# Attention and mixture of experts on one core: the second half of k is prepared one tile later, and the mask product reads PSUM

## The chip, the cores and the metric

The kernel runs on one core of a Trainium2 chip. The metric is the device time of one execution in microseconds (us).

The engines are named as the profile names them. PE is TensorE, DVE is VectorE, ACT is ScalarE, POOL is GpSimd, and SP is the engine whose queue issues most of the DMAs.

## The reference

Four batches, eight heads, 768 positions and 64 numbers a head go through local attention, and the result through a mixture of four experts.

```python
scores = scale * np.matmul(q, k.transpose(0, 1, 3, 2))          # q, k, v: (4, 8, 768, 64)
keep = is_global | is_local                                     # 8 first positions, or 96 behind
scores = np.where(keep, scores + bias, -1000000000.0)
a = softmax(scores)
x = (a @ v) as (4 * 768, 512)
p = domain_probs / (domain_probs.sum(-1, keepdims=True) + 1e-09)
for e in range(4):
    h = np.maximum(x @ w1[e], 0.0)                              # 512 -> 1024
    out += p[:, e:e + 1] * (h @ w2[e])                          # 1024 -> 512
```

## The kernel before

**The stages.** The attention of batch 0 runs first. Then the experts of batches 0 and 1 run (`first` and `second`), and beside them the attention of batches 1, 3 and 2 (`attention_chain`), whose instructions are put between those of the experts. From about 705 us on only the experts of batches 2 and 3 are left (`late_batch`).

**The unit of attention.** `attention_chain` goes through 12 pairs of heads, four for each of its three batches. A pair has six tiles of 128 queries. The chain is a generator that yields after each step, and a line near the end of the kernel (`count, span = ...`) paces it: the steps are spread evenly over the steps of the experts. A step is a call of `flow`, which is a pipeline four tiles deep. A tile enters with its scores (`scores`, four products into a tile of `ps`); one step later comes its softmax up to the exponential, and two steps later its normalisation to `pn` (both in `softmax`); three steps later it is turned (`turn_folded`: two or three transposes of `pn` into a PSUM tile `pt`, which are then copied to `pT` in SBUF). Once the sixth tile of a pair has been turned, the next step multiplies all six `pT` with v and vg (`weigh`, twice: 10 products into one `pt` tile for tiles 0 to 2, and 12 into another for tiles 3 to 5, each copied out by ACT as `x` or `piece`). There are 22 such products a pair, each half as wide as the array; they are counted here as 44, as the trace counts them.

**Other uses of `pt`.** q and k of a pair come in halves of three tiles. `prepare_q` and `prepare_k` transpose a half into a `pt` tile (three transposes), ACT copies it out and DVE takes what is left of it. The half of k with tiles 3 to 5 is needed from the scores of tile 3 on. All of this shares two PSUM buffers: `pt` has `bufs=2`, and the results of `weigh` lie in the same pool.

**The order.** While the attention chain runs, the framework's scheduler may reorder the instructions of each engine (`Ordered.on = False`); it works from its own costs. On the chip each engine then takes its own instructions strictly in that order, and a semaphore wait holds all that stands behind it.

**The experts.** `first` makes seven products (`pm<-xT,w1s`, `pm<-xB,w1s`, six matmuls of 384 columns each) for a unit of hidden features, and `second` six (`pm<-w2s,h`, six matmuls of 512 columns each). DVE adds them up, ACT makes the ReLU (`h`). The weights of a unit come by DMA (`raw`), and ACT and POOL split them into high and low parts (`w1s`, `w2s`); for batch 0 POOL also makes sums of them.

Of the kernel before, what the change touches and what calls it, by code (L numbers as in the profile page):

```python
# [14 lines left out]
ALU = mybir.AluOpType  # L15
# [3 lines left out]
P = 128  # L19
# [3 lines left out]
NPREV = 96  # L23
# [163 lines left out]
def attn_moe_kernel(ctx: ExitStack, tc, q, k, v, n_global, n_local, domain_probs, w1, w2, out):  # L187
# [4 lines left out]
    NQT = S // P  # L192
    NPAIR = H // 2
# [16 lines left out]
    ve, ac, po, sy, te = (Ordered(tc, e) for e in (nc.vector, nc.scalar, nc.gpsimd, nc.sync, nc.tensor))  # L210
# [11 lines left out]
    LATE = 2  # L222
# [9 lines left out]
    newer = fast.tile([P, P + NGLOB], BF16, name="newer")  # L232
# [177 lines left out]
    def scores(A, t, got):  # L410

        both = A.ps.tile([P, 2, 2 * P], F32, name="ps")
        c0 = (NQT - 1 - t) * PL - (0 if t else NPREV)
        for j in range(2):
            win = got["k"][:, j].rearrange("p t c -> p (t c)")[:, c0 : c0 + 2 * P]
            for part in range(2):
                te.matmul(
                    both[:, j],
                    got[("q", t // TPH)][:, j, part, t % TPH * P : (t % TPH + 1) * P],
                    win,  # L420
                    start=(part == 0),
                    stop=(part == 1),
                )
        return both
# [93 lines left out]
    def turn_folded(A, tile_):  # L518

        t, pn = tile_["t"], tile_["pn"]  # L520
        pt = A.pt.tile([P, 4, P], F32, name="pt")
        pT = tile_["pT"] = A.pT.tile([P, 2, 2, P], F32, name="pT")
        for place, at in enumerate((0, PL + NGLOB, P)[: 3 if t else 2]):
            te.transpose(pt[:, place, :], pn[:, at : at + P], ident)
        if t:
            for j in range(2):
                ac.copy(pT[NPREV:, 0, j], pt[j * NGLOB : (j + 1) * NGLOB, 2])
        ac.copy(pT[:, 1], pt[:, :2])
        if t:
            ve.scalar_tensor_tensor(  # L530
                pT[:NPREV, 0], newer[:NPREV, None, :P].to_broadcast([NPREV, 2, P]), 1.0, pT[:NPREV, 1],
                op0=ALU.subtract, op1=ALU.mult,
            )

    def weigh(A, three, x, b):

        px = A.px.tile([P, 512], F32, name=A.pxname)
        for i, tile_ in enumerate(three):
            t, pr, pT = tile_["t"], tile_["pr"], tile_["pT"]
            vt, vg = tile_["v"]["v"], tile_["v"]["vg"]  # L540
            parts = (1,) if t == 0 else (0, 1) if A.early else (1, 0)
            for w in parts:
                for j in range(2):
                    vv = vt[:, j, t] if w == 1 else vg[:, j, t - 1]
                    te.matmul(
                        px[j * D : (j + 1) * D, i * P : (i + 1) * P],
                        vv,
                        pT[:, w, j, :],
                        start=(w == parts[0]),
                        stop=(w == parts[-1]),  # L550
                    )
        cols = slice((t - TPH + 1) * P, (t + 1) * P)
        if x is not None:
            ac.copy(x[:, pr, cols], px[:, :HALF])
        else:
            piece = A.st.tile([P, HALF], F32, name="piece")
            ac.copy(piece, px[:, :HALF])
            ac.dma_start(xd[b][:, pr, cols], piece)
# [84 lines left out]
    def attention_chain(bs, A):  # L643

        tiles, turned = [None] * 4, []
        order = [(b, pr) for b in bs for pr in PAIRS]
        nats, gots = [{} for _ in order], [{} for _ in order]

        def flow(new=None):

            one, two, three, four = tiles
            if new:
                new["both"] = scores(A, new["t"], gots[new["m"]])
                new["ps"] = [new["both"][:, j] for j in range(2)]
            if four:
                turned.append(four)
            if len(turned) == NQT:
                b = order[four["m"]][0]
                for half in (turned[:TPH], turned[TPH:]):
                    weigh(A, half, xs[b], b)  # L660
                turned.clear()
            if three:
                turn_folded(A, three)
            softmax(A, one, two)
            tiles[:] = [new, one, two, three]

        def fetch_heads(m, names):

            if m < len(order):
                for n in names:  # L670
                    nats[m][n] = next(load(A, {"q": q, "k": k, "v": v}[n], *order[m], n))

        fetch_heads(0, "qkv")
        yield
        prepare_q(A, nats[0]["q"], 0, gots[0])
        flow()
        yield
        spread_q(0, gots[0])
        for m, (b, pr) in enumerate(order):
            if pr == PAIRS[0]:  # L680
                xs[b] = None if b == B - 1 else xp.tile([P, NPAIR, S], F32, name="x")
                if b == B - 1:
                    xd[b] = dp.tile([P, NPAIR, S], F32, name="x_last")
            nat, got = nats[m], gots[m]
            for part, hf in ((prepare_k, 0), (prepare_q, 1)):
                part(A, nat[part.__name__[-1]], hf, got)
                flow()
                yield
            for t in range(NQT):
                if t == 1:  # L690
                    prepare_k(A, nat["k"], 1, got)
                if t == 4 and m + 1 < len(order):
                    prepare_q(A, nats[m + 1]["q"], 0, gots[m + 1])
                if t in (1, 2, 4):
                    flow()
                    if t == 2 and m:
                        fetch_heads(m, "v")
                    yield
                flow({"t": t, "pr": pr, "m": m, "v": nat})
                if t == 0:  # L700
                    spread_q(1, got)
                elif t == 1:
                    fetch_heads(m + 1, "q")
                elif t == 3:
                    fetch_heads(m + 1, "k")
                elif t == 4:
                    if m + 1 < len(order):
                        spread_q(0, gots[m + 1])
                    nat["vg"] = differences(A, nat["v"])
                yield  # L710
        while any(tiles):
            flow()
            yield
# [201 lines left out]
    per = E * NPR  # L915
# [524 lines left out]

    SUMUNITS = tuple(per + i for i in (0, 1, 3, 4, 5, 7, 8, 9, 11, 12, 13))
    todo_t = [units[i][1:] for i in range(per)]
    count, span = 3 * NPAIR * (5 + NQT) + 6, (LATE * 13 * per - 12) * 0.97
    emitted = done = paced = 0
    Ordered.on = True
    for _ in first_sums(1):
        work_chores()
    chores.append(first_splits())
    att = attention_chain((1, 3, 2), A)
    begin = 30  # L1450
    for b in range(LATE):
# [89 lines left out]
```

## Time and profile before

| | |
|---|---|
| median of 3 runs | 1172.14 us (1171.06 to 1173.47) |
| the profiled execution | 1172.39 us, its span 1170.6 us |
| PE busy | 1141.7 us, 98% of the span |
| DVE, ACT, POOL busy | 887.0, 635.9, 628.8 us |
| granted PE clock over the span | 0.997 |

The span runs from the first to the last instruction that the profile shows; 1.8 us of the profiled execution lie around it. The ends of PE's matmuls are modelled, so a busy PE may still be waiting; the starts of the matmuls are what is read below.

### The profile page before, as it was taken

The numbers are of one execution on the slowest core, as the hardware profiler recorded it, in microseconds if no ns is written. First come the engines' busy times: TensorE is split into PE (matmuls) and PEld (weight loads), VectorE is DVE, ScalarE is ACT, GpSimd is POOL, SyncE is SP. The second block draws the span as 40 slices with busy tenths as digits, with TensorE's granted clock in tenths as the row PEclk, the third lists the DMA queues.
The fourth block names the chain that finished last, engine by engine and source line by source line (L and its number), as shares of the span: only waits on it lengthen the run. The fifth ranks groups of instructions, "written<-read, shape, count | busy, mean of one in ns | idle before, by whom it ended". The sixth has DMA issues, their size and how long they took to land.

```text
span 1170.6 us, 21402 instructions
## 1 busy us (share of the span) xinstructions
PE 1141.7 (98%) x7414; PEld 1054.6 (90%) x7414; DVE 887.0 (76%) x2065; ACT 635.9 (54%) x1801; POOL 628.8 (54%) x609
## 2 busy tenths in 40 slices
PE   7899899999999999999999999999999999999997
PEld 5679788988888989888888989999999999999997
DVE  7977678777868877887787677777777777777776
ACT  6844777777753656666575324444444544444443
POOL 5676555645543224313222337777877855555554
PEclk9999999999999999999999999999999999999999
DMA  9558868678786898968857668888888687776763
GB/s 185 147 156 284 289 194 309 235 228 237 249 280 227 271 257 278 278 220 257 260 187 238 224 217 311 306 302 304 294 295 293 236 297 244 249 251 243 248 229 132
DMA packets 180978, 290.80 MB, mean 248 GB/s; under 512 B 86784, under 2 KB 137472, under 8 KB 168576
## 3 DMA queue, kind: packets, MB, share of 16 engines
q1 hardware_dynamic: 172992, 273.63, 70.3%
q10 hardware_dynamic: 7872, 15.74, 4.5%
q8 instruction: 61, 1.00, 0.4%
q14 instruction: 53, 0.43, 0.1%
HBM read 207.93 MB, written 70.78 MB: 238 GB/s over the span
## 4 chain that ended last, share of the span: by engine, by line
PE 80%; DVE 7%; ACT 6%; POOL 3%; issue 2%; DMA 2%; ACTq 0%; SPq 0%; DVEq 0%; POOLq 0%
PE pm L43 32%; PE pf L43 19%; PE X L43 11%; PE Y L43 9%; PE pt L43 5%; PE ps L43 3%; ACT pb L43 1%; POOL w1s L43 1%; DVE pb L43 1%; DMA raw<-in_moe_w_dram 1%; ACT pT L43 1%; POOL w2s L43 1%; DVE qd L43 1%; DVE pT L43 1%; POOL sums L43 1%
## 5 line engine op out<-in xcount | busy, mean ns | idle before, releaser
L43 PE MATMUL pm<-w2s,h 128*128 128x512 f32 x1152 | 283.2, 396 | 3.1 <-DVE h L43 2.1
L43 PEld LDWEIGHTS pm<-w2s,h 128*128 128x128 f32 x1152 | 210.7, 188 | 49.1 <-DVE h L43 4.5
L43 ACT ACTIVATE hf<-pf 128x384 f32<-128x384 f32 x128 | 62.8, 492 | 248.6 <-DVE pf L43 247.4
L43 POOL TENSOR_TENSOR hS<-sf,hS 128x384 fp32r<-128x384 f32 x126 | 134.3, 1084 | 112.8 <-ACT hS L43 112.1
L43 DVE SCALAR_TENSOR_TENSOR acc<-pm,prob,acc 128x512 f32<-128x512 f32 x180 | 133.2, 746 | 43.1 <-PE pm L43 40.9
L43 PE MATMUL pm<-xT,w1s 128*128 128x384 f32 x744 | 149.3, 341 | 0.0
L43 PE MATMUL pf<-xT,w1s 128*128 128x384 f32 x768 | 146.5, 335 | 0.9 <-ACT hf L43 0.7
L43 PEld LDWEIGHTS pf<-xT,w1s 128*128 128x128 f32 x768 | 131.3, 188 | 1.7 <-ACT hf L43 1.2
L43 PEld LDWEIGHTS pm<-xT,w1s 128*128 128x128 f32 x744 | 127.7, 188 | 0.1
L43 POOL TENSOR_TENSOR sums<-raw 128x256 f32<-128x256 f32 x54 | 39.0, 741 | 161.3 <-DMA raw<-in_moe_w_dram 121.9
L43 DVE TENSOR_TENSOR hA<-hf,hA 128x384 fp32r<-128x384 f32 x94 | 85.0, 930 | 50.5 <-ACT hA L43 50.5
L43 ACT ACTIVATE pb<-pb,nmax 128x160 f32<-128x160 f32 (+2 forms) x192 | 84.4, 447 | 67.0 <-DVE nmax L43 63.7
L43 PE MATMUL pm<-xB,w1s 128*128 128x384 f32 x574 | 119.8, 346 | 0.1
L43 PE MATMUL pf<-xB,w1s 128*128 128x384 f32 x576 | 110.7, 335 | 0.2 <-ACT hf L43 0.2
L43 PEld LDWEIGHTS pm<-xB,w1s 128*128 128x128 f32 x574 | 99.7, 188 | 6.1 <-issue 1.5
L43 PEld LDWEIGHTS pf<-xB,w1s 128*128 128x128 f32 x576 | 98.7, 188 | 0.5 <-ACT hf L43 0.4
L43 POOL TENSOR_TENSOR sf<-hf 128x384 f32<-128x384 f32 x63 | 70.3, 1116 | 44.0 <-ACT hf L43 44.0
L43 ACT ACTIVATE h<-pm 128x384 fp32r<-128x384 f32 x128 | 61.6, 492 | 57.9 <-DVE pm L43 55.3
L43 ACT COPY pT<-pt 128x256 f32<-128x256 f32 (+2 forms) x216 | 71.1, 329 | 20.0 <-PE pt L43 13.1
L43 ACT ACTIVATE pn<-pb,zsum 128x32 f32<-128x32 f32 (+3 forms) x228 | 71.1, 368 | 17.6 <-DVE zsum L43 16.6
L43 PE MATMUL X<-w2b,hS 128*128 128x256 f32 x576 | 74.0, 282 | 0.0
L43 PE MATMUL Y<-w2b,hS 128*128 128x256 f32 x576 | 74.0, 282 | 0.0
(168 smaller groups left out, 2260.0 us busy)
## 6 DMA issues: line engine op xcount, KB each, us to landing
w1s<-kept SPq DMA_DIRECT2D x47, 1792.0 KB, 8.7
w2b<-kept SPq DMA_DIRECT2D x224, 256.0 KB, 4.4
kept<-w1s SPq DMA_DIRECT2D x16, 1792.0 KB, 7.5
raw<-in_moe_w_dram SPq DMA_DIRECT2D x43, 512.0 KB, 4.7
kept<-w2s SPq DMA_DIRECT2D x16, 1024.0 KB, 9.0
w2s<-kept SPq DMA_DIRECT2D x16, 1024.0 KB, 5.8
qd<-qd ACTq DMA_DIRECT2D x48, 192.0 KB, 6.2
q<-in_q_dram SPq DMA_DIRECT2D x30, 192.0 KB, 6.9
```

What stands on the lines that cost most here:

```text
L43: ins = fn(*args, **kwargs)
```

## The change

Three edits go together. In `attention_chain` the second half of k is prepared ahead of tile 2 and no longer ahead of tile 1, and the extra step that stood ahead of tile 1 is dropped: a pair has ten steps and no longer eleven. `count` in the pacing line follows (from 5 + 6 to 4 + 6 steps a pair). In `turn_folded` the mask product (`newer` minus 1, times the transposed weights) reads the PSUM tile `pt` and no longer the copy `pT`, and stands ahead of ACT's copies.

```diff
@@ turn_folded
         if t:
+            ve.scalar_tensor_tensor(
+                pT[:NPREV, 0], newer[:NPREV, None, :P].to_broadcast([NPREV, 2, P]), 1.0, pt[:NPREV, :2],
+                op0=ALU.subtract, op1=ALU.mult,
+            )
             for j in range(2):
                 ac.copy(pT[NPREV:, 0, j], pt[j * NGLOB : (j + 1) * NGLOB, 2])
         ac.copy(pT[:, 1], pt[:, :2])
-        if t:
-            ve.scalar_tensor_tensor(
-                pT[:NPREV, 0], newer[:NPREV, None, :P].to_broadcast([NPREV, 2, P]), 1.0, pT[:NPREV, 1],
-                op0=ALU.subtract, op1=ALU.mult,
-            )
@@ attention_chain
             for t in range(NQT):
-                if t == 1:
+                if t == 2:
                     prepare_k(A, nat["k"], 1, got)
                 if t == 4 and m + 1 < len(order):
                     prepare_q(A, nats[m + 1]["q"], 0, gots[m + 1])
-                if t in (1, 2, 4):
+                if t in (2, 4):
                     flow()
                     if t == 2 and m:
                         fetch_heads(m, "v")
@@ pacing
-    count, span = 3 * NPAIR * (5 + NQT) + 6, (LATE * 13 * per - 12) * 0.97
+    count, span = 3 * NPAIR * (4 + NQT) + 6, (LATE * 13 * per - 12) * 0.97
```

**The products with v, on PE.** The rows are those of one pair (the ninth of twelve weigh steps), before the change. `pt<-pT,v` and `pt<-pT,vg` are the products of `weigh`, `pt<-ident,k` the transposes of the second half of k, and `pm<-xB` a product of the experts.

```order
L43 MATMUL pt_6651<-ident_58,k_6345 128x128 x3
L43 MATMUL pt_6659<-pT_6249,v_6261 64x128 x2
L43 MATMUL pt_6659<-pT_6329,v_6261 64x128 x2
L43 MATMUL pt_6659<-pT_6329,vg_6441 64x128 x2
L43 MATMUL pt_6659<-pT_6425,v_6261 64x128 x2
L43 MATMUL pt_6659<-pT_6425,vg_6441 64x128 x2
L43 MATMUL pm_6692<-xB22_4569,w1s_6092 128x384 x5
L43 MATMUL pt_6671<-pT_6471,v_6261 64x128 x2
L43 MATMUL pt_6671<-pT_6471,vg_6441 64x128 x2
L43 MATMUL pt_6671<-pT_6569,v_6261 64x128 x2
L43 MATMUL pt_6671<-pT_6569,vg_6441 64x128 x2
L43 MATMUL pt_6671<-pT_6613,v_6261 64x128 x2
```

The same pair on PE in the changed kernel:

```order
L43 MATMUL pt_6656<-pT_6273,v_6234 64x128 x2
L43 MATMUL pt_6656<-pT_6313,v_6234 64x128 x2
L43 MATMUL pt_6656<-pT_6313,vg_6431 64x128 x2
L43 MATMUL pt_6656<-pT_6415,v_6234 64x128 x2
L43 MATMUL pt_6656<-pT_6415,vg_6431 64x128 x2
L43 MATMUL pt_6668<-pT_6460,v_6234 64x128 x2
L43 MATMUL pt_6668<-pT_6460,vg_6431 64x128 x2
L43 MATMUL pt_6668<-pT_6561,v_6234 64x128 x2
L43 MATMUL pt_6668<-pT_6561,vg_6431 64x128 x2
L43 MATMUL pt_6668<-pT_6613,v_6234 64x128 x2
L43 MATMUL pt_6668<-pT_6613,vg_6431 64x128 x2
L43 MATMUL pm_6692<-xB22_4569,w1s_6092 128x384 x6
```

Before, three transposes of k stand ahead of the first half, and five matmuls of the experts (four in the second to the fifth pair) stand between the halves. After, all 22 products stand together; the transposes of k come 12 to 18 matmuls of the experts behind them, and between the last transposes of `pn` (the sixth tile's) and them lie 10 to 18 matmuls of the experts and the four of the scores of tile 1. Before, 11 of the 12 pairs were split in this way (the last pair, which has no successor, was not); after, none is.

**The first pair, on ACT.** `pb,zsum<-pb,nmax` is the exponential of one head of a tile, `pn<-pb` its normalisation, and `w1s<-raw` the split of weights that a DMA brings. Before:

```order
L43 CAST kd<-pt 64x3x128 x2
L43 ACTIVATE pb,zsum<-pb,nmax 128x128
L43 CAST w1s<-raw_1591 128x512
L43 CAST w1s<-raw_1591 128x256
L43 CAST w1s<-sums 128x512
L43 ACTIVATE pb,zsum<-pb,nmax 128x128
L43 CAST w1s<-sums 128x512
L43 ACTIVATE zsum<-zsum 128x2
L43 ACTIVATE pn<-pb,zsum 128x96
L43 ACTIVATE pn<-pb,zsum 128x32
```

After:

```order
L43 ACTIVATE pb,zsum<-pb,nmax 128x128 x2
L43 ACTIVATE zsum<-zsum 128x2
L43 ACTIVATE pn<-pb,zsum 128x96
L43 ACTIVATE pn<-pb,zsum 128x32
L43 CAST kd<-pt 64x3x128 x2
L43 ACTIVATE pb,zsum<-pb,nmax 128x160 x2
L43 ACTIVATE pn<-pb,zsum 128x96
L43 ACTIVATE pn<-pb,zsum 128x32
L43 ACTIVATE zsum<-zsum 128x2
L43 CAST w1s<-raw_1591 128x512
```

Both exponentials of the first tile and its normalisation now stand ahead of the split of `raw_1591`; before, the second exponential stood behind three instructions that need this DMA.

**The mask product and the copies, on ACT and DVE.** The names in brackets are the engines whose semaphores an instruction waits for. These are ACT's rows for the sixth tile of the same pair as above, before:

```order
L43 DMA qd_6563<-qd_6563 64x768 [waits DMAHW6_49,Activation_49]
L43 COPY pT_6613<-pt_6612 32x128 [waits PE_49]
L43 COPY pT_6613<-pt_6612 32x128
L43 COPY pT_6613<-pt_6612 128x256
L43 ACTIVATE pb_6687,zsum_6686<-pb_6687,nmax_6685 128x128 [waits DVE_49] x2
```

And after:

```order
L43 DMA qd_6555<-qd_6555 64x768 [waits DMAHW7_49,Activation_49]
L43 COPY pT_6613<-pt_6612 32x128 [waits DVE_49]
L43 COPY pT_6613<-pt_6612 32x128
L43 COPY pT_6613<-pt_6612 128x256
L43 ACTIVATE pb_6684,zsum_6683<-pb_6684,nmax_6682 128x128 [waits DVE_49] x2
```

The wait has turned round: ACT's copies waited for PE, and DVE's product for ACT (`pT_6613<-newer_87,pT_6613 96x256 [waits Activation_49]`); now DVE's product waits for PE alone, and ACT's copies wait for DVE. The number of instructions is the same on every engine.

## Rows read from the trace of the kernel before

**Rows 1.** Stretches: start:end, length, busy time (instructions) of PE, PEld, DVE, ACT, POOL, PEclk, DMA

```profile
120.00:705.00 585.00, 574.94 (x3473) 512.54 (x3472) 454.17 (x1092) 365.42 (x1131) 234.58 (x221) 1.00 0.77 247
705.00:1140.00 435.00, 434.10 (x3069) 433.31 (x3070) 315.69 (x558) 187.82 (x449) 301.30 (x278) 1.00 0.77 273
```

**Rows 2.** Waits of PE from 120 to 705 us: total us, times, longest us

```profile
PE pt L43 <- ACT pn L43: 3.5, 3, 3.2
PE pt L43 <- ACT x L43: 2.0, 3, 0.7
...
PE pt L43 <- DVE kd L43: 1.0, 2, 0.7
```

**Rows 3.** Timeline of PE, last pair: start us, us, engine line op, out<-in, shapes, count

```profile
650.79 0.66 PE L43 MATMUL pt<-pT,v 128*64 128x128 f32 x8
...
653.35 1.33 PE L43 MATMUL pm<-xB,w1s 128*128 128x384 f32 x6
```

**Rows 4.** Timeline of PE, third pair, of batch 1

```profile
239.45 0.66 PE L43 MATMUL pt<-pT,v 128*64 128x128 f32 x8
...
240.69 1.20 PE L43 MATMUL pm<-w2s,h 128*128 128x512 f32 x4
...
243.29 0.50 PE L43 MATMUL pm<-w2s,h 128*128 128x512 f32 x1
```

**Rows 5.** Timeline of PE, seventh pair, of batch 3

```profile
447.02 0.66 PE L43 MATMUL pt<-pT,v 128*64 128x128 f32 x8
...
450.88 0.44 PE L43 MATMUL pm<-xB,w1s 128*128 128x384 f32 x1
```

**Rows 6.** Timeline of PE, ninth pair; in brackets idle before, and its releaser

```profile
527.73 1.21 PE L43 MATMUL pm<-xB,w1s 128*128 128x384 f32 x6
...
528.78 0.49 PE L43 MATMUL pt<-ident,k 128*128 128x128 f32 x3
529.20 0.66 PE L43 MATMUL pt<-pT,v 128*64 128x128 f32 x8
...
530.45 1.14 PE L43 MATMUL pm<-xB,w1s 128*128 128x384 f32 x5
...
532.27 0.44 PE L43 MATMUL pt<-pT,v 128*64 128x128 f32 x4 [0.68 <-ACT x L43]
...
533.73 0.44 PE L43 MATMUL pm<-xB,w1s 128*128 128x384 f32 x1
```

**Rows 7.** Timeline of the other engines around the ninth pair's products

```profile
526.87 0.91 ACT L43 COPY pT<-pt 32x128 f32<-32x128 f32 x3 [0.53 <-PE pt L43]
...
527.08 2.39 POOL L43 TENSOR_TENSOR sums<-sums,raw 128x1024 fp32r<-128x1024 f32 x1
...
528.41 1.34 DVE L43 SCALAR_TENSOR_TENSOR pT<-newer,pT 96x256 f32<-96x256 bf16 x1
...
530.26 0.96 ACT L43 ACTIVATE h<-pm 128x384 fp32r<-128x384 f32 x2 [0.47 <-DVE pm L43]
...
531.74 0.48 ACT L43 COPY x<-pt 128x384 f32<-128x384 f32 x1
```

**Rows 8.** Timeline of ACT and PE in the first pair

```profile
112.76 8.46 PE L43 MATMUL pm<-w2s,h 128*128 128x512 f32 x36 [0.32 <-DVE h L43]
...
118.59 0.93 ACT L43 CAST w1s<-raw 128x512 fp32r<-128x512 f32 x2 [3.06 <-DMA raw<-in_moe_w_dram]
...
124.38 0.33 PE L43 MATMUL pt<-ident,pn 128*128 128x128 f32 x1 [3.17 <-ACT pn L43]
```

**Rows 9.** Tile pT from 120 to 705 us: duration ns min/median/max; who waited for it

```profile
L43 DVE SCALAR_TENSOR_TENSOR pT<-newer,pT x60: 409/422/1350, 132.5 to 648.7; 96x256 f32<-96x256 bf16 x60
...
  DVE pT L43: 6.1, 14
```

**Rows 10.** Groups of DVE from 120 to 705 us: count, busy us, mean ns

```profile
L43 DVE SCALAR_TENSOR_TENSOR acc<-pm,prob,acc 128x512 f32<-128x512 f32 x170 | 125.8, 746 | 40.5 <-PE pm L43 38.7
L43 DVE SCALAR_TENSOR_TENSOR h<-pm,h 128x384 fp32r<-128x384 f32 x112 | 60.6, 550 | 5.3 <-ACT h L43 4.2
```

## The prediction

> **What bounds the kernel now.** I read the stretches first, then PE's waits, then PE's timeline around the products with v. From 120 to 705 us, where the attention chain runs beside the experts, PE is busy for 574.94 of 585 us; from 705 to 1140 us, where the experts are alone, for 434.10 of 435 [rows 1]. DVE, the next busiest, has 454.17 of the 585 us. So PE is the bound in both, and the change touches only the first. Nothing behind 705 us waits for more than PE's turn, so that each microsecond that PE saves ahead of it comes off the end. That PE does the same matmuls before and after means that only its waits and its breaks can change.
>
> The waits shown are few: 3.5 us for `pn`, nearly all in one place, 2.0 us for `x`, 1.0 us for `kd` [rows 2]. But a busy PE hides some, since the ends are modelled; so I take distances between starts. In the one pair whose 22 products with v stand together, 2.56 us go by from the first of them (650.79) to the next matmul of the experts (653.35) [rows 3]. That is the price of an unbroken block, and I measure the broken ones against it.
>
> **The change, part by part.**
>
> **The products with v in one block.** A broken block holds four or five matmuls of the experts, which must be taken off. Six of 384 columns start at 527.73 and the next instruction at 528.78 [rows 6], so one takes 0.175 us; 36 of 512 columns took 8.46 us [rows 8], one 0.235. Three kinds of broken block show:
> - The first five pairs: 239.45 to 243.29 is 3.84 us [rows 4]; less four at 0.235 (0.94) it is 2.90, so 0.34 us over the unbroken one. It is PE's break between products half as wide as the array and full ones, which a broken block pays twice.
> - The sixth and the seventh pair: 447.02 to 450.88 is 3.86 us [rows 5], less five at 0.175 (0.88) 2.98: 0.42 over.
> - The eighth to the eleventh pair: 529.20 to 533.73 is 4.53 us [rows 6], less 0.88, 3.65: 1.09 over. Here the second half waits 0.68 us for ACT's copy of the first [rows 6], which stands behind a ReLU that waits for DVE and so comes at 531.74 [rows 7].
>
> Together 5 x 0.34 + 2 x 0.42 + 4 x 1.09 = 6.9 us. In the changed kernel the halves have a buffer each, with no transposes of k between, and all eleven are unbroken, so the term is 6.9 us if neither half waits. The first half's buffer is that of the fifth tile, a whole step old. The second half's is that of the sixth tile. Between its transposes and the second half stand at least 10 matmuls of the experts (1.75 us or more), four of the scores and the first half (1.25 us, 529.20 to 530.45, [rows 6]): about 3.5 us. What must be done in it: DVE's mask product (0.42) and ACT's three copies (0.91, [rows 7]), 1.3 us, and what these engines have in hand, about one instruction each (0.75 us for the longest on DVE, [rows 10]; 0.96 us for two ReLUs on ACT, [rows 7]): 3.0 us. It fits, with little to spare. I take 6.9; if it doesn't fit, the bounds are 0 and what the second halves wait now.
>
> **The first pair.** PE stands still for 3.17 us at 124.38 for the first tile's `pn`. ACT was waiting for a DMA of weights (3.06 us idle before 118.59, [rows 8]), and the second head's exponential stood behind that. In the changed order ACT has that exponential and the normalisation ahead of the split, and PE has the transposes two products of the experts and a set of scores later. So this wait goes: 3.2 us (the bounds are 0, if ACT is held by something else there, and 3.5, all that PE waits for `pn` [rows 2]).
>
> **The step moved.** The three transposes of k, ACT's two copies and DVE's two subtractions are the same number as before and now stand 12 to 18 matmuls behind the products with v. The second half of k is first needed by the scores of tile 3, two steps on, so that nothing is late. The DMAs of k and v are issued by SP one step earlier or later than before, as its queue goes; the loads of k wait for the transposes just moved, and the next pair needs them four steps later, some 16 us (two pairs take 529.20 less 447.02, 82.2 us [rows 5, 6], so one 41.1, and it has ten steps). I cost this at 0. The cover is those 16 us; were it gone, PE would wait for part of a load once a pair. The waits for `kd` (1.0 us in two places [rows 2]) come from the two buffers being wanted by k, q and `pn` in quick succession; in the first of these places more matmuls lie between after the change: 0.3 us saved, between 0 and 0.7.
>
> **The mask product.** It has no price in the trace with PSUM as its source. From SBUF it takes 0.409 us at the least [rows 9]; a product of DVE's that is half as wide again and reads PSUM takes 0.550 [rows 10]. So it is between 0.41 and 0.55, and I take 0.42, since the nearest row is the same shape. DVE is not the bound. What it gains is elsewhere: in 528.41 it took 1.34 us, beside an instruction of POOL's from 527.08 to 529.47 [rows 7], and up to 1.35 elsewhere [rows 9], against a median of 0.42. With one of its inputs in PSUM it should stay near 0.42, as DVE's products for `h`, which read PSUM, stay at 0.55 over 112 of them [rows 10]. That is part of why the second halves come late in the four worst pairs, so it is no further term.
>
> The Trainium skill has a rule for it ("SBUF — State Buffer", Who interferes with whom): a VectorE instruction with two SBUF inputs and a GpSimd instruction that reads SBUF shut each other out for the whole instruction, and one with a single SBUF input doesn't. By that rule the 1.34 us is a wait for POOL, and the trace agrees, since the product ends 0.28 us after POOL's does. By it alone, with the block left broken, four pairs would gain at most 0.67 us each (1.09 less 0.42), 2.7 us in all; the sum above doesn't need it.
>
> **The wait turned round.** ACT's three copies now wait for DVE, 60 times; before, DVE waited for ACT, 6.1 us in 14 places [rows 9]. Behind the copies on ACT stand exponentials and ReLUs, for which PE waits in the end. No row shows what it costs: below, nothing (ACT is idle for 219.6 of the 585 us [rows 1]); above, the 6.1 us that it cost on the other side, handed on whole. I take 0.5, near the lower end, since of the 6.1 us that DVE lost none shows among PE's waits.
>
> **The sum.** 6.9 + 3.2 + 0.3 - 0.5 = 9.9 us. The profiled execution took 1172.4 us (span 1170.6 and 1.8 around it), 0.3 over the median of the runs. 1172.4 - 9.9 = **1162.5 us**.
>
> **The rivals.**
> - *The first pair's wait stays, or one of its size comes elsewhere.* The order on all engines is new, and the old one had put that DMA's work ahead of the exponential. Against it: the exponential now stands ahead. It gives 1162.5 + 3.2 = 1165.7.
> - *The second halves wait for the sixth tile's buffer.* The margin is 3.5 us against 3.0. If it is missed by 0.5 us in eleven pairs, 5.5 us are given back: 1168.0. The same time comes out if the turned wait costs the whole 6.1 us (5.6 more than I took): 1168.1.
> - *Slower: ACT held by DVE.* The mask product now stands between PE's transposes and ACT, 60 times. If each holds ACT for an accumulation of DVE's (0.75, [rows 10]) and the product (0.42) and a fifth of that reaches PE, it is 60 x 0.23 = 14 us, 3.6 more than the gain of 10.4: 1176.0. It decides from 10.4 / 60 = 0.17 us a tile on. Against it: ACT is idle for a third of the stretch, and the copies stand in an order that already has DVE's product ahead of them. The Trainium skill gives this rival its reason ("PSUM — Partial Sum Buffer", PSUM bank collisions raise a hardware error): the chip does not arbitrate between two engines on one bank, so the program must keep ACT and DVE apart with semaphores. No run here shows a collision, and the wait stands in ACT's order, so the rule says that two readers of one `pt` cannot overlap; how much that costs is open.
> - *The change doesn't do what it says.* The order rules it out: all eleven blocks are whole.
>
> **How the numbers follow.** My forecast 0.55; the first rival 0.20; the second 0.15; slower 0.05; more than forecast 0.05 (all of the waits for `x` and `kd` and the smaller ones gone besides, some 3 us: 1159.5). The range reaches from 1158.5 to 1168.5: it takes in both rivals on this side and leaves out the slower case and the tails of the others. A measurement of this kernel can tell some 0.2% (2.3 us) from no change. Faster by more than that is below 1169.8, which all but the slower case and the worst of the second rival give: 0.91. Within it 0.05 (that worst, and a slower case that just makes up for the gain), slower 0.04.
>
> **What would show it.** The products with v should stand in one block of 2.56 us in all twelve pairs with no wait in them; PE's 3.17 us for `pn` near 124 should be gone; the mask product should take some 0.42 us everywhere, beside POOL too; the idle time of ACT before `pT<-pt` that DVE ends should be a few microseconds; and PE should pass from the attention to the experts alone about 10 us sooner. The prediction is wrong if PE's waits for `pt` come back under other names (ACT's copies, `x`), if a DMA holds ACT at another place, or if ReLUs behind ACT's copies make PE wait for `h`.

## The result and the profile after

The changed kernel takes 1159.12 us (median of 4 runs, 1156.80 to 1159.56), the kernel before 1172.26 us beside it (1171.06 to 1173.47). The ratio is 0.9884, with a 95% interval of 0.9867 to 0.9901. In the profiled executions the span fell from 1170.6 to 1157.8 us, by 12.8 us. The forecast was 9.9 us, 1162.5 us. So the direction was right, the time lies within the range given, and 2.9 us more came off than the sum had.

The stretches of the changed kernel (start:end, length, then busy time of PE, PEld, DVE, ACT, POOL, the granted clock of PE as a share, DMA) answer to [rows 1]. The attention now ends some 13 us sooner:

```profile
120.00:692.00 572.00, 568.42 (x3472) 514.80 (x3471) 442.50 (x1086) 359.36 (x1124) 233.71 (x223) 1.00 0.80 252
692.00:1127.00 435.00, 434.09 (x3070) 433.29 (x3069) 315.72 (x559) 187.44 (x448) 301.59 (x279) 1.00 0.78 273
```

The second stretch is as long and as full as before; the whole gain lies in the first. PE's waits in it (total us, times, longest) answer to [rows 2]:

```profile
PE pm L43 <- DVE h L43: 1.3, 2, 0.9
PE pt L43 <- ACT pn L43: 0.8, 2, 0.6
```

The waits for `x` (2.0 us) and `kd` (1.0 us) are gone, and of those for `pn` 0.8 of 3.5 us are left. PE's timeline around a block of products with v, in the seventh and in the ninth pair, shows it whole (to be laid beside [rows 5] and [rows 6]):

```profile
439.21 0.66 PE L43 MATMUL pt<-pT,v 128*64 128x128 f32 x8
...
441.76 1.31 PE L43 MATMUL pm<-xB,w1s 128*128 128x384 f32 x6
...
518.47 0.63 PE L43 MATMUL ps<-kd,qd 128*128 128x256 f32 x4
519.03 0.66 PE L43 MATMUL pt<-pT,v 128*64 128x128 f32 x8
...
521.58 1.31 PE L43 MATMUL pm<-xB,w1s 128*128 128x384 f32 x6
```

From its first product to the next matmul of the experts either block takes 2.55 us; the forecast had 2.56. None of the twelve holds a wait. In the first pair, PE's and ACT's timelines read as follows (to be laid beside [rows 8]):

```profile
116.20 0.39 ACT L43 ACTIVATE pb<-pb,nmax 128x128 f32<-128x128 f32 x1
...
117.30 0.59 ACT L43 ACTIVATE pn<-pb,zsum 128x96 f32<-128x96 f32 x2 [0.38 <-DVE zsum L43]
...
120.17 0.61 ACT L43 CAST w1s<-raw 128x512 fp32r<-128x512 f32 x1
...
121.85 0.38 PE L43 MATMUL pt<-ident,pn 128*128 128x128 f32 x2
```

The second exponential and the normalisation stand ahead of the cast of the weights, the cast waits for no DMA any more when its turn comes, and PE's transposes of `pn` start without a wait. The mask product, by tile `pT` (duration in ns, least, median and most), and what waited longest at that tile (us, times), answer to [rows 9]:

```profile
L43 DVE SCALAR_TENSOR_TENSOR pT<-newer,pt x60: 403/408/418, 126.4 to 634.6; 96x256 f32<-96x256 bf16 x60
...
  ACT pT L43: 45.2, 42
```

It takes 0.40 to 0.42 us in all 60 places. But ACT now stands still until it is done, 45.2 us in 42 places, where the prediction had "a few microseconds".

### The profile page after: what moved, and what is told of

Same layout as the page of the kernel before. It is cut to its first block, busy times and chain, and to the rows that moved or that the text cites. A ratio compares the mean times of both kernels' runs of the same rounds, so it can differ in the third digit from the quotient of the medians.

```text
span 1157.8 us, 21421 instructions
## 1 busy us (share of the span) xinstructions
PE 1133.1 (98%) x7414; PEld 1055.8 (91%) x7414; DVE 876.8 (76%) x2065; ACT 630.6 (54%) x1801; POOL 626.9 (54%) x609
## 4 chain that ended last, share of the span: by engine, by line
PE 85%; DVE 7%; ACT 4%; issue 1%; POOL 1%; DMA 1%; ACTq 0%; DVEq 0%
PE pm L43 37%; PE pf L43 19%; PE X L43 11%; PE Y L43 9%; PE pt L43 6%; PE ps L43 3%; DVE pb L43 1%; ACT pb L43 1%; ACT pT L43 1%; DVE qd L43 1%; DVE acc L43 1%; DVE xB L43 1%; DVE u L43 0%; DVE hA L43 0%; PE px L43 0%
## 5 line engine op out<-in xcount | busy, mean ns | idle before, releaser
L43 PE MATMUL pm<-xB,w1s 128*128 128x384 f32 x574 | 116.8, 344 | 0.6 <-DVE u L43 0.6
L43 ACT COPY pT<-pt 128x256 f32<-128x256 f32 (+2 forms) x216 | 70.7, 327 | 58.3 <-DVE pT L43 45.2
```

The lines of the kernel that those rows point to most:

```text
L43: ins = fn(*args, **kwargs)
```

## The experiments

Two theories went in. The first is that of the prediction: whole blocks and the first pair carry the gain, the mask product next to nothing. Its main rival was that the source of the mask product carries a good part. Later experiments ask how much each of the two carries, and what the turned wait costs. The runs were made in three groups, each on a chip of its own with the kernel before beside it, whose medians were 1171.8, 1172.1 and 1172.1 us. The ratio behind each time is that to the kernel before on the same chip, with its 95% interval.

**The order alone.** The changed kernel with the mask product as before, from SBUF and behind ACT's copies.

```diff
-                if t == 1:
+                if t == 2:
                     prepare_k(A, nat["k"], 1, got)
...
-                if t in (1, 2, 4):
+                if t in (2, 4):
...
-    count, span = 3 * NPAIR * (5 + NQT) + 6, ...
+    count, span = 3 * NPAIR * (4 + NQT) + 6, ...
```

> Before with the order alone changed: second half of k behind the second tile, ten steps a pair; DVE's mask product still reads SBUF behind ACT's copies. First theory (the whole blocks of products with v are worth some 7.4 us, the first pair's wait some 3.5, small waits the rest; the source of the mask product next to nothing): 1159 to 1161 us. Rival (the mask product out of PSUM carries a good part of it, since it keeps its 0.42 us beside POOL): 1163 to 1166 us, and PE waits for x or pn again.

Measured: 1161.29 us, 0.9906 (0.9892 to 0.9921), between the two bands. The sum of the prediction without its terms for the mask product gives 1162.0 us for this kernel, so these terms stand; against the kernel before beside it the gain is 10.5 us, where they add up to 10.4. All blocks are whole. But the mask product collides more in this order than before. DVE's group of it (count, busy us, mean ns, idle time before), in the kernel before and then in this one:

```profile
L43 DVE SCALAR_TENSOR_TENSOR pT<-newer,pT 96x256 f32<-96x256 bf16 x60 | 32.2, 537 | 7.2 <-ACT pT L43 6.1
```

```profile
L43 DVE SCALAR_TENSOR_TENSOR pT<-newer,pT 96x256 f32<-96x256 bf16 x60 | 38.1, 636 | 11.0 <-ACT pT L43 9.0
```

Of the 60 products of this kernel 21 took more than 0.45 us, of those of the kernel before 17. Each of them began while an instruction of POOL's was running and ends 0.28 to 0.29 us behind it. The timeline of this kernel shows what such a long product leads to:

```profile
541.55 1.01 DVE L43 SCALAR_TENSOR_TENSOR h<-pm,h 128x384 fp32r<-128x384 f32 x2
...
542.33 2.39 POOL L43 TENSOR_TENSOR sums<-sums,raw 128x1024 fp32r<-128x1024 f32 x1
542.87 2.13 DVE L43 SCALAR_TENSOR_TENSOR pT<-newer,pT 96x256 f32<-96x256 bf16 x1 [0.30 <-ACT pT L43]
...
544.92 0.55 DVE L43 TENSOR_TENSOR pm<-pm,vv 128x384 f32<-128x384 f32 x1
...
551.61 1.13 DVE L43 TENSOR_TENSOR kd<-pt,kd 64x384 fp32r<-64x384 f32 x2 [0.46 <-ACT kd L43]
...
552.88 0.56 PE L43 MATMUL pt<-ident,pn 128*128 128x128 f32 x3 [1.12 <-DVE kd L43]
```

The product ends at 545.00, 0.28 us behind POOL's instruction (544.72). DVE's accumulations behind it come late, so do its subtractions of k, and PE waits 1.12 us for the `pt` buffer that these still read. In the kernel that differs only in the source of the product ("The product from PSUM, behind the copies", below), PE's same three transposes start without a wait:

```profile
540.28 1.01 DVE L43 SCALAR_TENSOR_TENSOR h<-pm,h 128x384 fp32r<-128x384 f32 x2
...
541.94 0.56 DVE L43 TENSOR_TENSOR pm<-pm,vv 128x384 f32<-128x384 f32 x1
...
550.05 0.52 PE L43 MATMUL pt<-ident,pn 128*128 128x128 f32 x3
```

Ahead of the product DVE is 1.27 us later here than there (541.55 against 540.28) and PE 1.28 (542.88 against 541.60, the scores). Behind it DVE is 2.98 us later (544.92 against 541.94), and PE's transposes are 2.83 us later (552.88 against 550.05). So of the 1.71 us that this one product added to DVE's lag, 1.55 have reached PE, though the wait shows only 1.12 of them.

**The mask product alone.** Before, with the product from PSUM and ahead of the copies; eleven steps.

```diff
         if t:
+            ve.scalar_tensor_tensor(pT[:NPREV, 0], newer[...], 1.0, pt[:NPREV, :2], ...)
             for j in range(2):
                 ac.copy(pT[NPREV:, 0, j], pt[j * NGLOB : (j + 1) * NGLOB, 2])
         ac.copy(pT[:, 1], pt[:, :2])
-        if t:
-            ve.scalar_tensor_tensor(pT[:NPREV, 0], newer[...], 1.0, pT[:NPREV, 1], ...)
```

> Before with the mask product alone changed: it reads PSUM and stands ahead of ACT's copies; eleven steps, blocks of products with v broken as before, first pair's order on ACT as before. First theory: the product takes some 0.42 us everywhere, the four blocks that waited 0.68 us for ACT gain at most that, PE's 3.2 us near 124 us stay: 1169.5 to 1172 us. Rival (the mask product carries a good part of the gain): 1167 us or less.

Measured: 1167.68 us, 0.9962 (0.9948 to 0.9975); again between the bands. The prediction bounded this at 2.7 us, the waits of the four late blocks. These waits do go: PE has none for `x` left here. But the gain is 4.1 us against the kernel before beside it (2.9 to 6.1 by the interval), so the product also held PE elsewhere; of the waits for `kd`, 0.3 us are left of 1.0 [rows 2]. This run turns the wait round as well, so that its gain is the product's less the cost of the turned wait. The first pair's wait is still there:

```profile
PE pt L43 <- ACT pn L43: 3.4, 4, 2.6
...
PE pt L43 <- DVE kd L43: 0.3, 1, 0.3
```

**The second half of k behind the products, in the same step.** Before, with two calls swapped.

```diff
             for t in range(NQT):
-                if t == 1:
-                    prepare_k(A, nat["k"], 1, got)
...
                 if t in (1, 2, 4):
                     flow()
+                    if t == 1:
+                        prepare_k(A, nat["k"], 1, got)
```

> Before with one swap: in the step ahead of the second tile the second half of k is prepared behind the products with v, not ahead of them; still eleven steps, mask product from SBUF. The blocks come out whole, but on ACT the second exponential of the first tile still stands behind the cast that waits for a weight's DMA. First theory: 1172.3 less 7.4 gives 1164.9 (1163.5 to 1165.5), with PE's 3.2 us near 124 us still there. Rival (the shorter pair of ten steps is what gains): 1170 us or more.

Measured: 1164.60 us, 0.9932 (0.9919 to 0.9945), as the first theory had it. The swap alone, with eleven steps and the product from SBUF, makes the blocks whole and is worth 7.2 us. What it doesn't do shows in PE's waits: 2.8 us for `pn` in the first pair, and 1.1 us for `x`, since the transposes of k now stand right behind the products and want a `pt` buffer that ACT has yet to copy out. The 7.2 us are a balance: this 1.1 is lost, and the 1.0 us for `kd` [rows 2] are gone besides.

```profile
PE pt L43 <- ACT pn L43: 2.8, 1, 2.8
...
PE pt L43 <- ACT x L43: 1.1, 2, 0.9
```

**The first pair alone.** Before, with the load of one set of weights issued two steps later, so that the exponential stands ahead of the cast.

```diff
-                    chores.append(... else load_w1(i + 2, wait))
+                    chores.append(... else load_w1(i + 2, 11 if i == 3 else wait))
```

> Before with one number changed: the load of the first weights of the sixth unit of the experts is issued two steps later, so that on ACT both exponentials of the first tile stand ahead of the cast that waits for it. All else is as before, the broken blocks too. First theory: PE's 3.2 us near 124 us go and nothing else, 1169.0 us (1168.5 to 1169.5). Rival (the wait comes elsewhere, PE waiting for the weights or pn a little later): 1171 to 1173 us.

Measured: 1169.12 us, 0.9976 (0.9963 to 0.9988), 2.7 us faster (1.4 to 4.3 by the interval). In the first pair PE now waits 0.80 us and not 3.17. It doesn't lose the whole of it since in this order the normalisation itself still stands behind the cast, as the timeline of ACT and PE shows; in the changed kernel it stands ahead of it too. So the wait came from ACT's order around one DMA.

```profile
116.40 0.40 ACT L43 ACTIVATE pb<-pb,nmax 128x128 f32<-128x128 f32 x1 [1.64 <-DVE nmax L43]
...
120.08 0.62 ACT L43 CAST w1s<-raw 128x512 fp32r<-128x512 f32 x1 [2.95 <-DMA raw<-in_moe_w_dram]
120.60 1.06 ACT L43 ACTIVATE pn<-pb,zsum 128x96 f32<-128x96 f32 x4
...
121.24 0.81 PE L43 MATMUL pt<-ident,pn 128*128 128x128 f32 x2 [0.80 <-ACT pn L43]
```

**The product from PSUM, behind the copies.** The changed kernel with the product put back behind ACT's copies, still reading `pt`; run twice, the second time on one chip with the changed kernel.

```diff
         if t:
-            ve.scalar_tensor_tensor(pT[:NPREV, 0], newer[...], 1.0, pt[:NPREV, :2], ...)
             for j in range(2):
                 ac.copy(pT[NPREV:, 0, j], pt[j * NGLOB : (j + 1) * NGLOB, 2])
         ac.copy(pT[:, 1], pt[:, :2])
+        if t:
+            ve.scalar_tensor_tensor(pT[:NPREV, 0], newer[...], 1.0, pt[:NPREV, :2], ...)
```

> The changed kernel with DVE's mask product put back behind ACT's copies, still reading PSUM. If what counts is where it reads (out of POOL's way, 0.42 us or less everywhere), it runs as the changed kernel: 1158.5 to 1160 us. Rival (what counts is its place, DVE first and ACT after): as the kernel with the order alone changed, 1161 us or more, and DVE waits for ACT's copies, ACT no longer for DVE's product.

Measured: 1157.60 us, 0.9873 (0.9859 to 0.9887): faster than the order alone by 3.7 us, and than expected. The two ran on different chips, but their ratios to the kernel before (0.9906 and 0.9873) have intervals that don't overlap. The place is not nothing, but its sign is the other one: DVE first is the worse. So the two were laid side by side.

> The changed kernel itself, on one chip with the next. Both theories: 1159.1 us, 0.9885 of before.

> The changed kernel with the mask product back behind ACT's copies, out of PSUM, on one chip with the changed kernel. If the turned wait (45.2 us in 42 places in which ACT stands for DVE) reaches PE, this one is 1.0 to 2.0 us faster than the changed kernel beside it, as the two profiles have it (1.75 us less of PE's time in longer distances between starts). Rival (ACT's wait is wholly covered, and the 1.5 us between the two medians are chance): within 0.5 us of it.

Measured: the changed kernel 1159.48 us (1158.26 to 1160.29), 0.9891 (0.9874 to 0.9908); with the product behind the copies 1157.61 us (1156.73 to 1157.70), 0.9877 (0.9857 to 0.9896). The ratios to before overlap, but the two kernels' runs on this chip don't, and the two medians of the second kernel agree. So the turned wait costs 1.9 us here, 1.5 by the medians of the first two measurements (1159.12 and 1157.60); one of the nine runs of the changed kernel, 1156.80, is as fast as the second kernel. In the profiles PE's waits for `pn` and `h` together are 2.1 and 1.5 us in the changed kernel, and 0.6 and 0.4 with the product behind the copies. A place where the turned wait reaches PE, from the timeline of the changed kernel:

```profile
265.88 0.99 DVE L43 CAST kd<-kd 128x384 fp32r<-128x384 f32 x1
...
266.79 1.13 DVE L43 SCALAR_TENSOR_TENSOR qd<-pt,qd 64x384 fp32r<-64x384 f32 x2
...
267.96 0.42 DVE L43 SCALAR_TENSOR_TENSOR pT<-newer,pt 96x256 f32<-96x256 bf16 x1
...
268.41 0.90 ACT L43 COPY pT<-pt 32x128 f32<-32x128 f32 x3 [2.46 <-DVE pT L43]
...
269.21 0.93 ACT L43 ACTIVATE pn<-pb,zsum 128x160 f32<-128x160 f32 x3
...
269.69 0.33 PE L43 MATMUL pt<-ident,pn 128*128 128x128 f32 x1 [0.55 <-ACT pn L43]
```

The product itself takes 0.42 us, but it stands on DVE behind a cast and two subtractions, so that ACT waits 2.46 us; behind ACT's copies stands the next tile's normalisation, and PE waits 0.55 us for that. With the product behind the copies PE has no wait for `pn` in the stretch, and DVE waits at `pT` instead of ACT, 6.6 us in 17 places (from that kernel's tile `pT`):

```profile
  DVE pT L43: 6.6, 17
```

**One input out of SBUF.** The order alone, with the mask product replaced by an instruction of one input. The mask is left out, in this kernel and in the next.

```diff
-            ve.scalar_tensor_tensor(pT[:NPREV, 0], newer[...], 1.0, pT[:NPREV, 1], ...)
+            ve.tensor_scalar(pT[:NPREV, 0], pT[:NPREV, 1], 1.0, 0.5, op0=ALU.subtract, op1=ALU.mult)
```

> The changed order with the mask product replaced by an instruction of DVE's that reads one SBUF tile and no mask (the mask is left out: a subtraction and a product with constants), in its old place behind ACT's copies. If two SBUF inputs beside POOL are what stretched the product to 1.3 to 2.1 us, this one stays under 0.5 us everywhere and PE's waits of 1.48 us near 148 and 1.29 near 551 us go: 1158.5 to 1160 us. Rival (the 2 us between the order alone and the whole change come from the place of the product or from the new order of PE): 1161 us or more.

Measured: 1161.38 us, 0.9907 (0.9894 to 0.9919), as the order alone. The instruction is shorter, 0.279 us at the least, and yet held up to 2.43 us. So that one of the inputs was the mask isn't what counts. In the longest case it ends at 545.53, 0.16 us behind POOL's (545.37):

```profile
L43 DVE TENSOR_SCALAR pT<-pT x60: 279/291/2427, 128.9 to 637.3; 96x256 f32<-96x256 f32 x60
...
542.98 2.39 POOL L43 TENSOR_TENSOR sums<-sums,raw 128x1024 fp32r<-128x1024 f32 x1
543.10 2.43 DVE L43 TENSOR_SCALAR pT<-pT 96x256 f32<-96x256 f32 x1 [0.30 <-ACT pT L43]
```

The two readings left were that this form takes the way that POOL uses for another reason, or that any of DVE's instructions out of SBUF is held. The same with an accumulator tells them apart.

```diff
+            ve.tensor_scalar(pT[:NPREV, 0], pT[:NPREV, 1], 1.0, None, op0=ALU.subtract, op1=ALU.add,
+                             accum_out=tile_["zsum"][:NPREV, :1])
```

> The changed order with the mask product replaced by a subtraction of DVE's that reads one SBUF tile and writes its sum to an accumulator as well (the mask is left out, and the sum falls on a value that is no longer needed), in the old place behind ACT's copies. If what stretches the instruction is that it takes a second way into SBUF that POOL uses, this form has none and stays under 0.5 us in all 60 places: 1157 to 1159 us. The Trainium skill (SBUF, State Buffer: Who interferes with whom) names this form of tensor_scalar as one that doesn't contend, and the plain form as one that can. Rival (any of DVE's instructions out of SBUF is held by POOL here): stretched beside POOL as the plain form was, 1161 us or more.

Measured: 1157.24 us, 0.9870 (0.9850 to 0.9890). The form with an accumulator reads the same tile out of SBUF, is slower by itself (0.403 us, and a read of the accumulator of 0.08 us behind each), and is never held:

```profile
L43 DVE TENSOR_SCALAR_CACHE_REDUCE pT<-pT x60: 403/416/418, 128.9 to 633.8; 96x256 f32<-96x256 f32 x60
```

So it isn't PSUM as such that helps; a form that POOL doesn't hold does as well out of SBUF, to within 0.4 us.

**The halves of a block in two steps.** The changed kernel with the first three tiles multiplied as soon as they are turned.

```diff
-            if len(turned) == NQT:
+            if len(turned) == TPH:
                 b = order[four["m"]][0]
-                for half in (turned[:TPH], turned[TPH:]):
-                    weigh(A, half, xs[b], b)
+                weigh(A, turned, xs[b], b)
                 turned.clear()
```

> The changed kernel with the products with v of each pair issued in two steps, the first three tiles as soon as they are turned, the last three where the block stands now; no transposes are added. First theory (each change between products half as wide as the array and full ones has its own price, 0.34 us for a second going in and out): 12 x 0.34 = 4.1 us, 1163.2 us (1162.5 to 1164). Rival (the broken block cost only its waits, and a break by itself next to nothing): 1160 us or less.

Measured: 1161.91 us, 0.9915 (0.9903 to 0.9928): 2.4 to 2.8 us over the changed kernel, two thirds of the 4.1 expected. A quiet pair of this kernel gives the price, on PE:

```profile
463.75 0.63 PE L43 MATMUL ps<-kd,qd 128*128 128x256 f32 x4
464.32 0.66 PE L43 MATMUL pt<-pT,v 128*64 128x128 f32 x8
...
465.56 0.55 PE L43 MATMUL pt<-ident,pn 128*128 128x128 f32 x3
...
477.30 0.64 PE L43 MATMUL ps<-kd,qd 128*128 128x256 f32 x4
477.77 0.49 PE L43 MATMUL pt<-ident,pn 128*128 128x128 f32 x3
...
481.25 0.63 PE L43 MATMUL ps<-kd,qd 128*128 128x256 f32 x4
...
483.27 1.31 PE L43 MATMUL pm<-xB,w1s 128*128 128x384 f32 x6
```

From the scores ahead to the next full matmul the halves take 1.81 and 2.02 us, 3.83 us; the whole block of the changed kernel takes 3.11 (518.47 to 521.58), and the second set of scores 0.47 (477.30 to 477.77 in this kernel, with transposes behind). So a second going in and out costs 0.25 us, and 0.30 if it is counted to the matmul behind the transposes (465.86 and 478.02), which are themselves slower behind the products. In three of the pairs (the second to the fourth) the second half is cut once more, behind its first product, so that there are 15 further breaks and not 12: at 0.25 us 3.8 us, of which 2.4 to 2.8 show in the time. Where the rest was won back stays open. But the break has a price of its own without any wait. The Trainium skill ("TensorEngine Tiling (Array Packing)", Key Properties) says that a change of the tiling mode drains TensorE, and gives no price; the 0.25 us agree with it, but no run shows the draining itself.

**Eleven steps, second half of k at the new place.** Two kernels. The first only moves `prepare_k` ahead of tile 2 and keeps the eleventh step; the second adds the product from PSUM behind the copies and the later load.

```diff
-                if t == 1:
+                if t == 2:
                     prepare_k(A, nat["k"], 1, got)
                 if t in (1, 2, 4):
                     flow()
```

> Before with the second half of k moved behind the second tile, but the step that it stood in kept, empty but for the flow of earlier tiles: eleven steps, mask product from SBUF. Blocks whole, on ACT the second exponential of the first tile still behind the cast that waits for a weight's DMA. First theory: as the kernel that only swaps the two inside the step, less the 1.5 us that its transposes of k wait behind the products with v: 1163 us (1162.5 to 1164.5), PE's 3 us near 124 us still there. Rival (ten steps are what gains beside the blocks): 1165 us or more with that wait gone; or as the ten steps, 1161 us, if the step's number is nothing and the first pair's wait goes by itself.

> Before with three edits: the second half of k behind the second tile with the eleventh step kept and empty, the mask product out of PSUM behind ACT's copies, and the load of the sixth unit's first weights two steps later. The order breaks the blocks of the first five pairs once, after five products, and leaves the others whole. First theory (blocks, the source of the mask product and the first pair are all there is; the number of steps is nothing): 1157.6 plus 5 x 0.35 us, 1159.4 us (1158.5 to 1160.5). Rival (ten steps have a gain of their own): 1161.5 us or more.

Measured: 1166.20 us, 0.9954 (0.9941 to 0.9967), and 1166.46 us, 0.9951 (0.9935 to 0.9967). Both miss what the first theory had, by 3 and by 7 us. For the first kernel the rivals as worded don't hold, since its wait in the first pair stays; for the second the rival's 1161.5 us or more holds. In the first kernel the blocks are whole and the wait in the first pair is there, as expected; its waits for DVE's `h` are 2.0 us and those for `pn` 4.1. In the second PE's waits are these:

```profile
PE pm L43 <- DVE h L43: 2.2, 4, 0.9
PE pt L43 <- ACT pn L43: 0.9, 2, 0.7
...
PE pt L43 <- DVE kd L43: 0.6, 1, 0.6
```

Against the ten steps with the product behind the copies (0.4 us for `h`, no others of these) this is 3.3 us. The five blocks that are cut after ten products of 44 cost more than I took: the second pair takes 4.49 us from its first product to the next matmul (192.66 to 197.15), less six at 0.235 us 3.08, so 0.52 over 2.56 and 2.6 us in five pairs. PE's timeline of this pair shows what is special about the place:

```profile
192.66 0.66 PE L43 MATMUL pt<-pT,v 128*64 128x128 f32 x8
193.15 0.38 PE L43 MATMUL pt<-pT,vg 128*64 128x128 f32 x2
...
195.04 0.32 PE L43 MATMUL pt<-pT,vg 128*64 128x128 f32 x1
195.05 0.32 PE L43 MATMUL pt<-pT,v 128*64 128x128 f32 x1
...
197.15 1.20 PE L43 MATMUL pm<-w2s,h 128*128 128x512 f32 x4
```

The products run in twos: the matmul of the second starts 0.01 us behind that of the first (195.04 and 195.05), and the next two follow 0.11 to 0.15 us later. A cut behind five products (ten matmuls, `x8` and `x2`) leaves an odd number on either side, so that one product in each part runs alone. The part of ten takes 0.80 us and that of 34 takes 2.11. Halves of ten and twelve products take 1.24 and 1.46 us, which is 0.055 us a matmul; at that price the two parts would take 0.69 and 2.01. So the odd cut costs some 0.2 us more than one between two pairs, an estimate from these four times.

Together 5.9 of the 8.4 us between the two spans (1163.3 and 1154.9). The rest is spread over PE's order and stays open, as does whether it is the number of steps or the transposes of k so near to those of `pn`. The number of steps alone can hardly be it: the kernel with the two calls swapped has eleven steps too, and 1164.60 us less its 2.8 in the first pair is 1161.8, next to the 1161.29 of the ten steps. What the two kernels settle is that with the second half of k at its new place the eleventh step is not free.

## Why the prediction was right, and where it was off

**The bound, the blocks and the first pair: right.** The gain lies wholly ahead of the stretch of the experts alone. The blocks came out whole at 2.55 us; the swap alone gave 7.2 us on balance where the term had 6.9. (The term counted five early pairs at 0.34 us. In the first of them five matmuls of the experts and a wait of 0.13 us lie between the halves, 156.75 to 161.01, which makes 0.53 by the same reckoning and the term 7.1.) The second halves do not wait for the sixth tile's buffer, so the second rival is out. The first pair's wait is gone and PE waits nowhere in the stretch longer than 0.9 us, which rules out the first rival, and changing only ACT's order around that DMA took 2.7 of the 3.2 us off. The order alone, 1161.29 us, is within 0.7 us of these terms' 1162.0.

**The price of a break: right for its place, and no constant.** The 0.34 us were read between matmuls of the experts, and the sum used them only there. Carried over to other places they missed: 0.25 to 0.30 us between scores and transposes, and 0.52 where the cut left an odd number of products on either side.

**The step that failed: "so it is no further term".** The mask product's source was costed at nothing beyond the four late blocks. With the blocks whole it is worth 3.7 us (1161.29 to 1157.60). The prediction saw that the product took 1.34 us beside POOL, and that DVE is not the bound, and stopped there; its 2.7 us for the product by itself counted only the waits at the products with v. What it left out is that the new order sets the product beside POOL's instructions at other times (38.1 us busy against 32.2), and that what stands behind it on DVE releases PSUM buffers, for which PE waits later and under other names: in the order alone 1.4 us for `kd` and 1.3 for `pT`, and nothing for either with the product from PSUM behind the copies. In the place shown the wait comes eight us later, and 1.55 of 1.71 us reach PE.

**The turned wait: right in kind, mis-sized.** I took 0.5 us, between 0 and 6.1; it measured 1.5 to 1.9. ACT's idle time before the copies is 45.2 us, not a few, since what ACT waits for isn't the product (0.42 us) but all that stands ahead of it on DVE. That nearly all of the 45.2 us cost PE nothing shows how much slack ACT had: 1.9 / 60 = 0.03 us a tile reach PE, far from the 0.17 from which the slower rival decides. The sign that the prediction names for it, waits of PE's for `h`, decides nothing: 1.3 and 0.3 us in two profiles of the changed kernel, 0.6 and 0.4 in two with the product behind the copies. The Trainium skill ("PSUM — Partial Sum Buffer", PSUM bank collisions raise a hardware error) asks that two engines be kept apart on one bank. No run here shows a collision; what the runs add is that the side that waits is a choice, 45.2 us of ACT's time one way round and 6.6 us of DVE's the other.

**The sum.** From the order alone to the changed kernel the two terms that were off give 3.7 less 1.9, a gain of 1.8 us, where the prediction had a loss of 0.5: 2.3 us of difference. The order alone came out 0.7 us below its terms' time. Together that is 3.0 us, where the spans gave 2.9 more than the forecast. These are the steps from one measured kernel to the next, so that they must add up to about that; what shows the causes are the runs and traces behind each step.

That the time lies within the range is in part luck. It came out 0.6 us above the lower end, 1158.5, and the two errors have opposite signs: without the cost of the turned wait, the gain that was left out would have taken the time below the range, to 1157.6 us.

The best version of the change that was run is ten steps with the product from PSUM behind ACT's copies, 1157.6 us.

## What to carry to other kernels

When an instruction off the bound takes three times its usual time beside another engine's, don't ask only who waits for it where it stands: ask what stands behind it in its queue, and which buffers that releases. A wait between two engines on one buffer is better laid so that the one with less work queued ahead goes first; here that was ACT, for 1.5 to 1.9 us. Products of half the array's width are worth keeping together even where nothing waits, here for 0.25 to 0.34 us a break, and a cut that can't be avoided belongs behind an even number of them (0.52 us where it didn't).

## What the runs showed of the hardware that was not expected

A DVE instruction with a single input out of SBUF was held by POOL just as one with two: the plain `tensor_scalar` took 0.279 us alone and up to 2.43 us beside POOL, to an end 0.16 us behind POOL's in the case shown. The same with an accumulator took 0.403 us and was never over 0.418. The Trainium skill ("SBUF — State Buffer", Who interferes with whom) lists the plain form among those that can take the port pair shared with GpSimd, and excepts the form that writes its accumulator; the two kernels agree with it, 2.43 against 0.418 us. The prediction told that section's rule without this exception, as if a single SBUF input were enough to be free. Here the slower instruction made the faster kernel, by 4.1 us (1161.38 to 1157.24).

Two products of half the array's width ran side by side: the starts of their matmuls are 0.01 us apart, and 24 matmuls take 0.22 us more than 20. A product that a cut left without its partner took about as long as two; the two odd parts above were 0.10 to 0.11 us longer than their number of matmuls makes.
